# Grouped attention on one core: wide transposes of query and key with a permuted row order, and V loaded dense and spread by GpSimd

## The chip, the cores and the metric

The kernel runs on one core of one Trainium2 chip. The core has five engines that run side by side and meet only at semaphores: TensorE (PE; its weight loads are listed apart as PEld), VectorE (DVE), ScalarE (ACT), GpSimd (POOL) and SyncE (SP), which here only issues DMAs. The metric is the device time of one execution in microseconds (us), as the median of several executions. Two versions of the kernel are told apart by the ratio of their medians.

## The reference

```python
B, Hq, Hkv, Sq, Sk, D = 16, 32, 8, 288, 512, 128      # bf16
def reference(q, k, v):
    k = jnp.repeat(k, Hq // Hkv, axis=1)
    v = jnp.repeat(v, Hq // Hkv, axis=1)
    scores = jnp.einsum("bhqd,bhkd->bhqk", q, k) * D ** -0.5
    p = softmax(scores, axis=-1)
    return jnp.einsum("bhqk,bhkd->bhqd", p, v)
```

Four query heads share one key/value head. So there are 16 x 8 = 128 independent groups, each with 4 x 288 = 1152 query rows against 512 keys of 128 numbers. The softmax is taken without subtracting a maximum; a flag at the end says whether the sums stayed in range, and a slow general path would run if they had not.

## The kernel before

The program goes through the 128 groups one after the other. Two sizes name everything: `NT = 9` is the number of 128-row tiles of the 1152 queries of a group, `NJ = 4` the number of 128-key tiles of its 512 keys.

**Loads.** Four groups make a unit (`UG = 4`, so 32 units), and three units fit in SBUF (`NSLOT = 3`). `op_load` (lines 377 to 399) issues three DMAs for a unit on the queue of SyncE: a transposing DMA for the keys (line 388), one for the queries (line 391), and a plain one for V (line 398). The transposes read rows of 128 numbers that lie one behind the other in HBM and leave, on 128 partitions (the 128 numbers of a row), the columns in the order of the rows: `qt_sb[:, slot, group, 0:1152]` and `kt_sb[:, slot, group, 0:512]`. The plain load writes V in pieces of 128 numbers (256 bytes) into rows of 160 (`VP = 160`), of which column 128 holds a one. From the fourth unit on, `op_load` first waits until the S products and the PV products of the unit that had the slot are done. The first unit is loaded in two parts, its first group by itself, so that work can begin early; its V comes behind the second part.

**S products.** The scores are made transposed: keys on partitions, queries along the free axis. For each group, 4 key tiles x 1152 queries make 4608 columns, cut into three steps of 1536 columns. `op_s` (line 429) does one step, by four matmuls of up to 512 columns whose weights are a 128x128 tile of `kt_sb` and whose moving operand is a stretch of `qt_sb`. The step's result fills one of two PSUM buffers `ps_s`.

**Exponentials.** `op_exp` (line 460) reads the 1536 columns of one step from `ps_s` and writes them, as bf16, to `pt_sb`, which holds three groups. There are 384 of these steps, all on ScalarE.

**PV products.** `op_pv` (line 447) does one third of a group: three query tiles, each the sum of four matmuls over the key tiles. Here the exponentials are the weights (128 keys x 128 queries), and V with its column of ones is the moving operand, 129 columns; column 129 of the result is the softmax's denominator. Because the output rows are stored as `(p t)`, so that each partition writes nine neighbouring rows, tile `t` takes the queries t, t+9, t+18, ... of the group, and the 128 weights of a row are read from `pt_sb` with a step of nine elements (line 446).

**Division and stores.** VectorE takes the reciprocals of the three denominators (line 468) and multiplies (line 480) into `o_sb`, which holds six groups. `op_store` (line 405) sends a finished group to HBM, on SyncE's queue again.

**Order.** TensorE's order is written out by hand: for each step n it does the S product of step n and then the PV product of step n - 4 (`LAG = NC + 1 = 4`). The S product of step n waits for the exponential of step n - 2 (its PSUM buffer), the PV product for its group's exponentials and for VectorE's emptying of its PSUM buffer. SyncE's order is a list sorted by keys, in which the loads of a unit come right after the PV products that free its slot and the stores between them. GpSimd has no work in this path.

Of the kernel before, what the change touches and what calls it, by code (L numbers as in the profile page):

```python
# [8 lines left out]
BF16 = mybir.dt.bfloat16  # L9
# [276 lines left out]
def bass_standalone__gqa_softmax__near_ridge_kernel(  # L286
# [5 lines left out]
):  # L292
    B, Hq, Sq, D = q.shape
    _, Hkv, Sk, _ = k.shape
    P = 128
    R = (Hq // Hkv) * Sq
    NJ = Sk // P
    NT = R // P
# [7 lines left out]
    NC = COLS // CH  # L306
    assert COLS % CH == 0 and NT % 3 == 0 and NC == NT // 3
    scale = float(D) ** -0.5
    DV = D + 1
    VP = 160  # L310
    LAG = NC + 1
    UG = 4
    NU = NG // UG
    NSLOT = 3
    NPT = 3
    NO = 6

    q_v = q.rearrange("b h s d -> (b h s) d")
    k_v = k.rearrange("b g s d -> (b g s) d")
    v_v = v.rearrange("b g (j p) d -> p (b g j) d", p=P)  # L320
    o_v = out.rearrange("b h s d -> (b h s) d").rearrange("(g p t) d -> g p (t d)", p=P, t=NT)

    with ExitStack() as es:
        sem = {}

        def S(name):
            if name not in sem:
                sem[name] = es.enter_context(nc.semaphore(name))
            return sem[name]

        flag_i = es.enter_context(nc.sbuf_tensor("flag_i", [1, 1], I32))
        block = es.enter_context(nc.Block())
        main = ExitStack()
        v_sb = main.enter_context(nc.sbuf_tensor("v_sb", [P, NSLOT, UG * NJ, VP], BF16))
        qt_sb = main.enter_context(nc.sbuf_tensor("qt_sb", [P, NSLOT, UG, R], BF16))
        kt_sb = main.enter_context(nc.sbuf_tensor("kt_sb", [P, NSLOT, UG, Sk], BF16))
        pt_sb = main.enter_context(nc.sbuf_tensor("pt_sb", [P, NPT, COLS], BF16))
        o_sb = main.enter_context(nc.sbuf_tensor("o_sb", [P, NO, NT, D], BF16))
        rl_sb = main.enter_context(nc.sbuf_tensor("rl_sb", [P, NG * NT], FP32))
# [3 lines left out]
        dum = main.enter_context(nc.sbuf_tensor("dum", [P, 2], FP32))  # L343
# [5 lines left out]
        def need(eng, waits):  # L349

            left = []
            for (s, n) in waits:
                key = (id(eng), s)
                if seen.get(key, 0) < n:
                    seen[key] = n
                    left.append((sem[s], n))
            return left

        def emit(eng, waits, fn):
            waits = need(eng, waits)  # L360
            for (s, n) in waits[:-1]:
                eng.wait_ge(s, n)
            ins = fn()
            if waits:
                ins.wait_op(waits[-1][0], waits[-1][1], "sem-ge")
            return ins

        for name in ["s_one", "s_s", "s_e", "s_pv", "s_rc", "s_ev", "s_stat", "s_bad", "s_flag", "s_go", "s_q0", "s_k0"]:
            S(name)
        for i in range(NSLOT):  # L370
            for name in ["s_q%d", "s_k%d", "s_v%d"]:
# [5 lines left out]
        def op_load(u, part=None):  # L377
            eng = nc.sync
            sl = u % NSLOT
            if u >= NSLOT:  # L380
                last = (u - NSLOT + 1) * UG - 1
                for (s, n) in need(eng, [("s_s", NC * (last + 1)), ("s_pv", NC * (last + 1))]):
                    eng.wait_ge(s, n)
            g0, g1 = {None: (0, UG), 0: (0, 1), 1: (1, UG)}[part]
            sq = sem["s_q0"] if part == 0 else sem["us_q%d" % sl]
            sk = sem["s_k0"] if part == 0 else sem["us_k%d" % sl]
            gg = u * UG
            eng.dma_start_transpose(  # L388
                kt_sb[:, sl, g0:g1].rearrange("d g c -> d (g c)"),
                k_v[(gg + g0) * Sk:(gg + g1) * Sk]).then_inc(sk, 16)  # L390
            eng.dma_start_transpose(  # L391
                qt_sb[:, sl, g0:g1].rearrange("d g c -> d (g c)"),
                q_v[(gg + g0) * R:(gg + g1) * R]).then_inc(sq, 16)
            if part != 0:
                if u == 0:
                    for (s, n) in need(eng, [("s_one", 1)]):
                        eng.wait_ge(s, n)
                eng.dma_start(
                    v_sb[:, sl, :, 0:D], v_v[:, gg * NJ:(gg + UG) * NJ]).then_inc(sem["us_v%d" % sl], 16)

        def op_store(g):
            eng = nc.sync
# [5 lines left out]
        def pieces(i):  # L408
            cuts = sorted({i * CH, (i + 1) * CH}
                          | {x for x in range(0, COLS, BANK) if i * CH < x < (i + 1) * CH}  # L410
                          | {x for x in range(0, COLS, R) if i * CH < x < (i + 1) * CH})
            return list(zip(cuts[:-1], cuts[1:]))

        def op_s(n):
            eng = nc.tensor
            g, i = n // NC, n % NC
            u, gi = g // UG, g % UG
            sl = u % NSLOT
            waits = []
            if g == 0:  # L420
                waits += [("s_k0", 16), ("s_q0", 16)]
            else:
                waits += [("us_k%d" % sl, 16 * (u // NSLOT + 1)), ("us_q%d" % sl, 16 * (u // NSLOT + 1))]
            if n >= 2:
                waits.append(("s_e", n - 1))
            ps = pieces(i)
            for x, (a, b) in enumerate(ps):
                j, r0 = a // R, a % R
                ins = emit(eng, waits if x == 0 else [], lambda: eng.matmul(  # L429
                    ps_s[:, n % 2, a - i * CH:b - i * CH],  # L430
                    kt_sb[:, sl, gi, j * P:(j + 1) * P],
                    qt_sb[:, sl, gi, r0:r0 + b - a], start=True, stop=True))
            ins.then_inc(sem["s_s"], 1)

        def op_pv(r):
            eng = nc.tensor
            g = r // NC
            u, gi = g // UG, g % UG
            sl = u % NSLOT
            waits = [("us_v%d" % sl, 16 * (u // NSLOT + 1)), ("s_e", NC * (g + 1))]  # L440
            if r >= 2:
                waits.append(("s_ev", r - 1))
            for a in range(3):
                t = 3 * (r % NC) + a
                for j in range(NJ):
                    w = pt_sb[:, g % NPT, j * R:(j + 1) * R].rearrange("k (p t) -> k t p", t=NT)[:, t]
                    ins = emit(eng, waits if a == 0 and j == 0 else [], lambda: eng.matmul(  # L447
                        ps_o[:, r % 2, a * DV:(a + 1) * DV], w,
                        v_sb[:, sl, gi * NJ + j, 0:DV],
                        start=(j == 0), stop=(j == NJ - 1)))  # L450
            ins.then_inc(sem["s_pv"], 1)


        def op_exp(n):
            eng = nc.scalar
            g, i = n // NC, n % NC
            waits = [("s_s", n + 1)]
            if g >= NPT:
                waits.insert(0, ("s_pv", NC * (g - NPT + 1)))
            emit(eng, waits, lambda: eng.activation(  # L460
                pt_sb[:, g % NPT, i * CH:(i + 1) * CH], ps_s[:, n % 2], ACTF.Exp, scale=scale)
            ).then_inc(sem["s_e"], 1)


        def op_rc(r):
# [40 lines left out]
        @block.sync  # L506
        def _(eng):
            for (_, fn) in sp:
                fn()
            for g in range(max(0, NG - NO), NG):  # L510
                for (s, n) in need(eng, [("s_o%d" % (g % NO), 16 * (g // NO + 1))]):
                    eng.wait_ge(s, n)
# [13 lines left out]
        def _(eng):  # L526
            emit(eng, [("s_one", 1)], lambda: eng.activation(dum[:, 1:2], dum[:, 0:1], ACTF.Exp))  # L527
            for n in range(NS):
                op_exp(n)

        @block.vector
        def _(eng):
            eng.memset(dum[:], 0.0)  # L533
            eng.memset(one_f[:], 1.0)
            eng.memset(v_sb[:, :, :, D:VP], 1.0).then_inc(sem["s_one"], 1)  # L535
            per_b = G * NC
            for r in range(NS):
                op_rc(r)
                op_ev(r)
                if r % per_b == per_b - 1:  # L540
                    op_stat(r // per_b)
            emit(eng, [("s_stat", B)], lambda: eng.tensor_reduce(  # L542
                ck_sb[:, 0:1], st_sb[:, 0, :], AX.X, ALU.max))
            eng.tensor_reduce(ck_sb[:, 1:2], st_sb[:, 1, :], AX.X, ALU.min).then_inc(sem["s_stat"], 1)  # L544
            emit(eng, [("s_stat", B + 1)], lambda: eng.tensor_scalar(  # L545
                out=ck_sb[:, 2:3], in0=ck_sb[:, 0:1], scalar1=SUM_MAX, scalar2=None, op0=ALU.is_gt)
            ).then_inc(sem["s_stat"], 1)
            emit(eng, [("s_stat", B + 2)], lambda: eng.scalar_tensor_tensor(  # L548
                out=ck_sb[:, 3:4], in0=ck_sb[:, 1:2], scalar=1.0 / SUM_MAX, in1=ck_sb[:, 2:3],
                op0=ALU.is_lt, op1=ALU.add)).then_inc(sem["s_bad"], 1)  # L550
            emit(eng, [("s_bad", 2)], lambda: eng.tensor_copy(flag_i[:], ps_s[0:1, 0, 0:1])  # L551
                 ).then_inc(sem["s_flag"], 1)
# [52 lines left out]
```

## Time and profile before

| what | us |
|---|---|
| median of 6 runs | 542.43 (542.10 to 543.21) |
| the profiled execution, its own time | 542.57 |
| its span, first to last instruction | 540.8 |
| ScalarE busy | 523.2 (97%) |
| TensorE busy (matmuls) | 520.6 (96%) |
| TensorE weight loads | 427.5 (79%) |
| VectorE busy | 290.2 (54%) |
| GpSimd busy | 0.2 (0%) |
| chain that ended last: share of PE lines 447 and 429 | 51% and 44% |

The granted TensorE clock was 0.996 over the span. A busy share is no proof of a bound: matmuls are pipelined, and an activation's recorded time overlaps the next one's, so that one engine can stand at 97% while it waits a little before every step. What bounds a step is read from the starts of the steps, which the timeline gives. Two rows of the transfers are worth having at hand too: the DMA queue of SyncE's transfers was busy for 88.2% of 16 engines' span, and 283200 of the 299650 packets had under 512 bytes.

### The profile page before, as it was taken

The numbers are of one execution on the slowest core, as the hardware profiler recorded it, in microseconds if no ns is written. First come the engines' busy times: TensorE is split into PE (matmuls) and PEld (weight loads), VectorE is DVE, ScalarE is ACT, GpSimd is POOL, SyncE is SP. The second block draws the span as 40 slices with busy tenths as digits, with TensorE's granted clock in tenths as the row PEclk, the third lists the DMA queues.
The fourth block names the chain that finished last, engine by engine and source line by source line (L and its number), as shares of the span: only waits on it lengthen the run. The fifth ranks groups of instructions, "written<-read, shape, count | busy, mean of one in ns | idle before, by whom it ended". The sixth has DMA issues, their size and how long they took to land.

```text
span 540.8 us, 13994 instructions
## 1 busy us (share of the span) xinstructions
PE 520.6 (96%) x6045; PEld 427.5 (79%) x6146; DVE 290.2 (54%) x808; ACT 523.2 (97%) x386; POOL 0.2 (0%) x4
## 2 busy tenths in 40 slices
PE   4999999999999999999999999999999999999994
PEld 1788888888888888888888888888888888888884
DVE  1455555555555555555555555555555555555554
ACT  4999999999999999999999999999999999999992
POOL 0000000000000000000000000000000000000000
PEclk9999999999999999999999999999999999999998
DMA  8999989988879997999989889998999889799211
GB/s 165 213 245 261 229 217 248 191 216 199 204 208 249 172 223 196 212 218 245 210 177 199 226 213 239 167 224 207 206 228 226 190 197 220 209 230 220 100 67 70
DMA packets 299650, 110.01 MB, mean 203 GB/s; under 512 B 283200, under 2 KB 283200, under 8 KB 299584
## 3 DMA queue, kind: packets, MB, share of 16 engines
q1 hardware_dynamic: 299584, 109.07, 88.2%
q8 instruction: 49, 0.80, 0.7%
q14 instruction: 17, 0.14, 0.1%
HBM read 16.78 MB, written 37.75 MB: 101 GB/s over the span
## 4 chain that ended last, share of the span: by engine, by line
PE 95%; DMA 1%; issue 1%; SPq 1%; DVE 1%
PE ps_o L447 51%; PE ps_s L429 44%; DMA qt_sb<-in_q_dram 1%; SPq L388 1%; DVE o_sb L480 0%; SPq L391 0%; DVE rl_sb L468 0%; PE ps_s L521 0%; DVE ck_sb L548 0%; DVE ck_sb L542 0%; DVE ck_sb L545 0%; DVE flag_i L551 0%; DVE st_sb L492 0%; DVE st_sb L490 0%; DVE ck_sb L544 0%
## 5 line engine op out<-in xcount | busy, mean ns | idle before, releaser
L460 ACT ACTIVATE pt_sb<-ps_s 128x1536 bf16<-128x1536 f32 x384 | 521.7, 1450 | 6.4 <-PE ps_s L429 6.4
L447 PEld LDWEIGHTS ps_o<-v_sb,pt_sb 128*128 128x128 bf16 x4608 | 333.0, 140 | 40.4 <-DMA v_sb<-in_v_dram 0.6
L447 PE MATMUL ps_o<-v_sb,pt_sb 128*128 128x129 bf16 x4608 | 334.5, 222 | 1.6 <-DVE o_sb L480 0.2
L429 PE MATMUL ps_s<-qt_sb,kt_sb 128*128 128x512 bf16 (+3 forms) x1435 | 297.6, 325 | 11.8 <-DMA qt_sb<-in_q_dram 7.6
L480 DVE TENSOR_TENSOR o_sb<-ps_o,rl_sb 128x384 bf16<-128x384 f32 x384 | 214.3, 558 | 13.5 <-DVE rl_sb L468 0.3
L468 DVE RECIPROCAL rl_sb<-ps_o 128x3 f32<-128x3 f32 x384 | 69.6, 181 | 230.8 <-PE ps_o L447 230.8
L429 PEld LDWEIGHTS ps_s<-qt_sb,kt_sb 128*128 128x128 bf16 x1536 | 131.6, 99 | 65.9 <-DMA qt_sb<-in_q_dram 6.1
L492 DVE TENSOR_REDUCE st_sb<-rl_sb 128x1 f32<-128x72 f32 x16 | 3.5, 218 | 0.0
L490 DVE TENSOR_REDUCE st_sb<-rl_sb 128x1 f32<-128x72 f32 x16 | 3.5, 218 | 0.0
L527 ACT ACT_TABLE_LOAD x1 | 1.3, 1283 | 0.8 <-PEq L590 0.8
L521 PE MATMUL ps_s<-ck_sb,one_f 128*1 128x1 f32 x2 | 0.2, 164 | 1.8 <-DVE ck_sb L548 1.8
L521 PEld LDWEIGHTS ps_s<-ck_sb,one_f 128*1 128x1 f32 x2 | 0.1, 80 | 1.9 <-DVE ck_sb L548 1.9
L535 DVE MEMSET v_sb<- 128x1536 bf16 x1 | 1.3, 1338 | 0.3 <-issue 0.3
L527 ACT ACTIVATE dum<-dum 128x1 f32<-128x1 f32 x1 | 0.2, 202 | 0.5 <-DVE v_sb L535 0.5
L533 DVE MEMSET dum<- 128x2 f32 x1 | 0.1, 60 | 0.9 <-PEq L590 0.9
L551 DVE CAST flag_i<-ps_s 1x1 int32<-1x1 f32 x1 | 0.1, 146 | 0.3 <-PE ps_s L521 0.3
L542 DVE TENSOR_REDUCE ck_sb<-st_sb 128x1 f32<-128x16 f32 x1 | 0.2, 170 | 0.0
L548 DVE SCALAR_TENSOR_TENSOR ck_sb<-ck_sb 128x1 f32<-128x1 f32 x1 | 0.2, 159 | 0.0
L545 DVE TENSOR_SCALAR ck_sb<-ck_sb 128x1 f32<-128x1 f32 x1 | 0.2, 153 | 0.0
L544 DVE TENSOR_REDUCE ck_sb<-st_sb 128x1 f32<-128x16 f32 x1 | 0.2, 158 | 0.0
L590 POOL MEMSET const-bfloat16-1.0<- 128x1 bf16 x1 | 0.1, 102 | 0.0
L590 POOL MEMSET const-uint8-127<- 128x1 uint8 x1 | 0.1, 101 | 0.0
(3 smaller groups left out, 0.3 us busy)
## 6 DMA issues: line engine op xcount, KB each, us to landing
out_dram<-o_sb SPq DMA_DIRECT2D x128, 288.0 KB, 4.4
v_sb<-in_v_dram SPq DMA_DIRECT2D x32, 512.0 KB, 5.2
kt_sb<-in_k_dram SPq DMA_TRANSPOSE x33, 4.8
qt_sb<-in_q_dram SPq DMA_TRANSPOSE x33, 8.1
```

Of the source, the lines that this page charges most:

```text
L388: eng.dma_start_transpose(kt_sb[:, sl, g0:g1].rearrange("d g c -> d (g c)"), k_v[(gg + g0) * Sk:(gg + g1) * Sk]).then_inc(sk, 16)
L429: ins = emit(eng, waits if x == 0 else [], lambda: eng.matmul(ps_s[:, n % 2, a - i * CH:b - i * CH], kt_sb[:, sl, gi, j * P:(j + 1) * P], ...
L447: ins = emit(eng, waits if a == 0 and j == 0 else [], lambda: eng.matmul(ps_o[:, r % 2, a * DV:(a + 1) * DV], w, v_sb[:, sl, gi * NJ + j, ...
L460: emit(eng, waits, lambda: eng.activation(pt_sb[:, g % NPT, i * CH:(i + 1) * CH], ps_s[:, n % 2], ACTF.Exp, scale=scale)).then_inc(sem["s_ ...
L468: emit(eng, [("s_pv", r + 1)], lambda: eng.reciprocal(rl_sb[:, 3 * r:3 * r + 3], src.rearrange("p a e -> p (a e)"))).then_inc(sem["s_rc"], 1)
L480: emit(eng, waits, lambda: eng.tensor_tensor(out=o_sb[:, g % NO, t0:t0 + 3, :], in0=src, in1=rl_sb[:, 3 * r:3 * r + 3].unsqueeze(2).broadc ...
L490: emit(eng, [("s_rc", (b + 1) * w // 3)], lambda: eng.tensor_reduce(st_sb[:, 0, b:b + 1], rl_sb[:, b * w:(b + 1) * w], AX.X, ALU.max))
L492: eng.tensor_reduce(st_sb[:, 1, b:b + 1], rl_sb[:, b * w:(b + 1) * w], AX.X, ALU.min).then_inc(sem["s_stat"], 1)
L521: emit(eng, [("s_bad", 1)], lambda: eng.matmul(ps_s[0:1, 0, 0:1], one_f[:], ck_sb[:, 3:4], start=True, stop=True)).then_inc(sem["s_bad"], 1)
L527: emit(eng, [("s_one", 1)], lambda: eng.activation(dum[:, 1:2], dum[:, 0:1], ACTF.Exp))
L535: eng.memset(v_sb[:, :, :, D:VP], 1.0).then_inc(sem["s_one"], 1)
L542: emit(eng, [("s_stat", B)], lambda: eng.tensor_reduce(ck_sb[:, 0:1], st_sb[:, 0, :], AX.X, ALU.max))
```

## The change

The rows of queries and keys are taken in another order, so that what the PV products read as weights lies together.

* The query rows of a group are numbered `x * 9 + t`. The source of the transposing DMA is now read as 128 rows for each group with 9 x 128 = 1152 numbers each, and the result is `qt_sb[:, slot, t, group, 0:128]`. For the keys it is 128 rows of 4 x 128 = 512 numbers, giving `kt_sb[:, slot, j, group, 0:128]`. The number of DMAs and their bytes stay.
* The S products read the moving operand as up to four stretches of 128 elements, one for each tile t.
* The PV weights are `pt_sb[:, ..., j * 1152 + t * 128 : ... + 128]`, 128 neighbouring elements.
* V is loaded into a new tile `vd_sb`, four neighbouring rows (1024 bytes) on each partition and group, and GpSimd copies it (`op_vc`, one copy for each unit, 32 in all) into `v_sb`, whose rows are now 129 wide. The PV products of a unit wait for this copy in place of the DMA.
* The loads of queries and keys of a unit no longer wait for the PV products of the unit that had the slot, only for its S products; the V load waits for the copy that empties `vd_sb`; the copy waits for the PV products that free `v_sb`.
* The column of ones is set by GpSimd, not by VectorE.

```diff
-    VP = 160
+    VP = DV
...
-    q_v = q.rearrange("b h s d -> (b h s) d")
-    k_v = k.rearrange("b g s d -> (b g s) d")
-    v_v = v.rearrange("b g (j p) d -> p (b g j) d", p=P)
+    q_v = q.rearrange("b h s d -> (b h s) d").rearrange("(x t) d -> x (t d)", t=NT)
+    k_v = k.rearrange("b g (p j) d -> (b g p) (j d)", j=NJ)
+    v_v = v.rearrange("b g (p j) d -> p (b g) (j d)", j=NJ)
...
+        vd_sb = main.enter_context(nc.sbuf_tensor("vd_sb", [P, NSLOT, UG, NJ * D], BF16))
         v_sb = main.enter_context(nc.sbuf_tensor("v_sb", [P, NSLOT, UG * NJ, VP], BF16))
-        qt_sb = main.enter_context(nc.sbuf_tensor("qt_sb", [P, NSLOT, UG, R], BF16))
-        kt_sb = main.enter_context(nc.sbuf_tensor("kt_sb", [P, NSLOT, UG, Sk], BF16))
+        qt_sb = main.enter_context(nc.sbuf_tensor("qt_sb", [P, NSLOT, NT, UG, P], BF16))
+        kt_sb = main.enter_context(nc.sbuf_tensor("kt_sb", [P, NSLOT, NJ, UG, P], BF16))
...
-                for (s, n) in need(eng, [("s_s", NC * (last + 1)), ("s_pv", NC * (last + 1))]):
+                for (s, n) in need(eng, [("s_s", NC * (last + 1))]):
...
             eng.dma_start_transpose(
-                kt_sb[:, sl, g0:g1].rearrange("d g c -> d (g c)"),
-                k_v[(gg + g0) * Sk:(gg + g1) * Sk]).then_inc(sk, 16)
+                kt_sb[:, sl, :, g0:g1].rearrange("d j g p -> d j (g p)"),
+                k_v[(gg + g0) * P:(gg + g1) * P]).then_inc(sk, 16)
             eng.dma_start_transpose(
-                qt_sb[:, sl, g0:g1].rearrange("d g c -> d (g c)"),
-                q_v[(gg + g0) * R:(gg + g1) * R]).then_inc(sq, 16)
+                qt_sb[:, sl, :, g0:g1].rearrange("d t g p -> d t (g p)"),
+                q_v[(gg + g0) * P:(gg + g1) * P]).then_inc(sq, 16)
             if part != 0:
-                if u == 0:
-                    for (s, n) in need(eng, [("s_one", 1)]):
+                if u >= NSLOT:
+                    for (s, n) in need(eng, [("s_vc", u - NSLOT + 1)]):
                         eng.wait_ge(s, n)
                 eng.dma_start(
-                    v_sb[:, sl, :, 0:D], v_v[:, gg * NJ:(gg + UG) * NJ]).then_inc(sem["us_v%d" % sl], 16)
+                    vd_sb[:, sl], v_v[:, gg:gg + UG]).then_inc(sem["us_v%d" % sl], 16)
...
-                    kt_sb[:, sl, gi, j * P:(j + 1) * P],
-                    qt_sb[:, sl, gi, r0:r0 + b - a], start=True, stop=True))
+                    kt_sb[:, sl, j, gi, :],
+                    qt_sb[:, sl, r0 // P:(r0 + b - a) // P, gi, :], start=True, stop=True))
...
-            waits = [("us_v%d" % sl, 16 * (u // NSLOT + 1)), ("s_e", NC * (g + 1))]
+            waits = [("s_vc", u + 1), ("s_e", NC * (g + 1))]
...
-                    w = pt_sb[:, g % NPT, j * R:(j + 1) * R].rearrange("k (p t) -> k t p", t=NT)[:, t]
+                    w = pt_sb[:, g % NPT, j * R + t * P:j * R + (t + 1) * P]
...
+        def op_vc(u):
+            eng = nc.gpsimd
+            sl = u % NSLOT
+            waits = [("us_v%d" % sl, 16 * (u // NSLOT + 1))]
+            if u >= NSLOT:
+                waits.append(("s_pv", NC * UG * (u - NSLOT + 1)))
+            emit(eng, waits, lambda: eng.tensor_copy(
+                v_sb[:, sl, :, 0:D], vd_sb[:, sl].rearrange("p g (j d) -> p (g j) d", d=D))
+            ).then_inc(sem["s_vc"], 1)
...
+        @block.gpsimd
+        def _(eng):
+            eng.memset(v_sb[:, :, :, D:DV], 1.0)
+            for u in range(NU):
+                op_vc(u)
+
         @block.vector
         def _(eng):
-            eng.memset(dum[:], 0.0)
+            eng.memset(dum[:], 0.0).then_inc(sem["s_one"], 1)
             eng.memset(one_f[:], 1.0)
-            eng.memset(v_sb[:, :, :, D:VP], 1.0).then_inc(sem["s_one"], 1)
```

## The prediction

> **What bounds the kernel now.** First the page: two engines stand at 96 and 97%, so the shares decide nothing. Its costliest groups give the durations.
>
> ```profile
> L460 ACT ACTIVATE pt_sb<-ps_s 128x1536 bf16<-128x1536 f32 x384 | 521.7, 1450 | 6.4 <-PE ps_s L429 6.4
> L447 PEld LDWEIGHTS ps_o<-v_sb,pt_sb 128*128 128x128 bf16 x4608 | 333.0, 140 | 40.4 <-DMA v_sb<-in_v_dram 0.6
> ...
> L429 PEld LDWEIGHTS ps_s<-qt_sb,kt_sb 128*128 128x128 bf16 x1536 | 131.6, 99 | 65.9 <-DMA qt_sb<-in_q_dram 6.1
> ```
>
> Weight loads with a step of nine elements (L447) take 140 ns, contiguous ones (L429) 99 ns. 384 exponentials at 1450 ns would be 557 us, more than the span of 540.8, so they overlap and their starts must be read. Second, the timeline of TensorE in mid-run (start, length):
>
> ```profile
> 250.97 0.89 PE L447 MATMUL ps_o<-v_sb,pt_sb 128*128 128x129 bf16 x12
> 251.70 0.81 PE L429 MATMUL ps_s<-qt_sb,kt_sb 128*128 128x384 bf16 x4
> 252.35 0.86 PE L447 MATMUL ps_o<-v_sb,pt_sb 128*128 128x129 bf16 x12
> 253.05 0.81 PE L429 MATMUL ps_s<-qt_sb,kt_sb 128*128 128x512 bf16 x4
> 253.70 0.86 PE L447 MATMUL ps_o<-v_sb,pt_sb 128*128 128x129 bf16 x12
> 254.39 0.81 PE L429 MATMUL ps_s<-qt_sb,kt_sb 128*128 128x512 bf16 x4
> ```
>
> From start to start, an S product holds TensorE for 0.65 us (251.70 to 252.35), the three PV products of a group for 0.73, 0.70 and 0.69 us. Steps are thus 1.38, 1.35 and 1.34 us, with no row of waiting between. Third, ScalarE at the same time, two neighbouring exponentials to a row; length less 1.45 is the distance of their starts.
>
> ```profile
> 251.17 2.83 ACT L460 ACTIVATE pt_sb<-ps_s 128x1536 bf16<-128x1536 f32 x2
> ...
> 252.55 2.80 ACT L460 ACTIVATE pt_sb<-ps_s 128x1536 bf16<-128x1536 f32 x2
> ```
>
> 1.38 and 1.35. The exponential at 252.55 starts 0.04 us after its S product ends (251.70 + 0.81 = 252.51): ScalarE waits for TensorE. In the long 1.38 step that wait is real. Fourth, the start of the run, where ScalarE once is not waiting:
>
> ```profile
> 6.14 2.74 PE L429 MATMUL ps_s<-qt_sb,kt_sb 128*128 128x512 bf16 x8 [6.14 <-DMA qt_sb<-in_q_dram]
> 7.63 2.79 ACT L460 ACTIVATE pt_sb<-ps_s 128x1536 bf16<-128x1536 f32 x2 [4.82 <-PE ps_s L429]
> ...
> 12.02 2.72 PE L429 MATMUL ps_s<-qt_sb,kt_sb 128*128 128x512 bf16 x8 [1.41 <-DMA qt_sb<-in_q_dram]
> 14.66 0.81 PEld L447 LDWEIGHTS ps_o<-v_sb,pt_sb 128*128 128x128 bf16 x12 [0.62 <-DMA v_sb<-in_v_dram]
> ```
>
> Both S products are done at 6.14 + 2.74 = 8.88, yet the second exponential starts at 7.63 + 2.79 - 1.45 = 8.97, 0.09 later instead of 0.04. So 1.34 (1.347 in the trace's nanoseconds) is ScalarE's own pace. The kernel stands on two bounds: one step in three is TensorE's (1.38), the other two are equal on both engines. The same rows show that the first PV product waits for V until 14.66.
>
> **What the change removes.** With contiguous weights, TensorE's step is 0.65 plus twelve matmuls of 129 columns. The S rows stream 1536 columns in 0.65 us, 0.423 ns a column, so twelve take 0.66 us if streaming alone counts: a step of 1.31. If the 99 ns load only brings the slow PV product down to the other two, it is 1.35. Either way ScalarE's 1.347 takes over as the bound. The timeline has 381 exponentials in one row of 517.49 us, (517.49 - 1.45) / 380 = 1.358 a step. The gain is 380 x (1.358 - 1.347) = 4.2 us; less 0.1 for a start-up step of 1.456 that the average holds and in which the first PV product made ScalarE wait (it returns below), 4.1. With TensorE's slower bound (1.35 throughout) it is about 3.0. I take 3.9, nearer ScalarE's pace, because the S rows' loads of 99 ns hide behind a matmul of only 128 columns there. The last four PV products come after the last exponentials; at 0.03 to 0.07 us each that is 0.1 more. Sum: -4.0.
>
> The page ScalarE: Activation LUTs of the Trainium skill (section What ACT_TABLE_LOAD costs) speaks against this: 186 ns + 0.833 ns an element, less 93 of overlap, would be 1372 ns a step, ScalarE alone would be slower than the present 1.358, and the sum would hold no gain at all. The recorded 1.347 decides.
>
> **What it adds.** GpSimd's copy of V, 128 x 2048 elements, is between the V load and the PV products, 32 times. For all but the first unit it is hidden: its unit is needed two units (2 x 16.3 us) after the load is issued, and the load lands in 5.2 us (median). Were that cover gone, each copy would cost its whole length. The first copy has no cover. Before, V was in at 14.62, that is 2.65 us after the queries of the first unit's second part (12.0). V's packets grow from 256 to 1024 bytes. The bounds are the 2.65 us of now, and the store rows: stores of 288 KB with 2304-byte packets, issued one behind the other, land 0.7 us apart (48.26, 48.96, 49.65), so 512 KB in 1.25, with the 0.4 us that V now lands after its last packets. I take 1.9 (landed at 13.9), between them and nearer the stores, whose rows are also long runs. The copy itself has no row on GpSimd. Nearest rows: VectorE's memset of 1536 bf16 elements in 1338 ns (0.87 ns each, so 1.8 us) and its multiply of 384 in 558 ns (1.45 ns, so 3.0 us). I take 2.4, the middle, since a copy reads like the one and writes like the other. V is ready at 16.3, 1.7 us later than 14.62. TensorE is in order: behind the waiting PV product stand S step 5 and with it exponential 5, which started at 16.30, or 1.63 after that PV product. It moves by 1.7, and since ScalarE is then the bound, nothing makes it up. Bounds: 13.65 + 1.8 gives +0.8; 14.62 + 3.0 gives +3.0.
>
> The page GPSIMD Engine Reference (section 3.1) has about 1.03 cycles an element at 1.2 GHz for such bodies, an estimate of 1.8 us for the copy and of +1.1 in place of +1.7.
>
> **What it moves.** Bytes and number of the transposes stay, but a 256-byte piece is now read every 2304 (queries) or 1024 bytes (keys). The transfers' rows:
>
> ```profile
> SPq L405 <- DVE o_sb L480: 129.6, 83, 3.7
> SPq L383 <- PE ps_o L447: 78.7, 27, 2.9
> SPq L388 <- PE ps_s L429: 35.1, 29, 2.8
> ...
> v_sb<-in_v_dram SPq DMA_DIRECT2D x32, 512.0 KB, 5.2
> qt_sb<-in_q_dram SPq DMA_TRANSPOSE x33, 8.1
> ```
>
> SyncE's queue waits 243 us for compute, 7.6 a unit, so transfers have room in mid-run. At the start they have none: S step 3 waits until 12.02 for queries issued at 5.00. Lower bound: the same packets at the same pace, 0 (a gain, at most the 1.41 us of that wait, is not excluded by any row). Upper: V's present load reads 256-byte pieces apart and took 2.33 us for 2048 packets, against 14.3 ns for 16 packets in a transpose (18.2 against 14.3, 1.27 times): 7.0 x 0.27 = +1.9 us. I take 0, since the transposes' own row is the nearest.
>
> The page DMA: Bandwidth & Descriptors (section Latency and other measured facts) speaks against it: 261 GB/s with a non-contiguous middle dimension, some 30% under 350 to 400 for a contiguous one. Here the contiguous one already moves 1.18 MB in an issue of 4.63 us, 255 GB/s; a further 30% would put 3.0 us on the start and the sum at 543.3.
>
> Costed at nothing: the loads' dropped wait for PV (they start four steps, 5.4 us, earlier in a queue that waits anyway; the stores behind them have six `o_sb` buffers); V's new wait for a copy two units old; the column of ones moved to GpSimd, 0.1 us beside the first loads; S reading stretches of 128 elements at the same column count. VectorE has 1.35 - 0.74 = 0.6 us of slack a step, should GpSimd's copies touch it.
>
> Sum against the profiled execution: 542.57 - 4.0 + 1.7 = 540.3. The median is 0.14 lower: 540.2.
>
> **Rivals.** (1) The transfers become the bound: slower. For: 88.2% of the DMA engines' time is taken, and 9 of those 14.4 us a unit are transposes (6656 packets x 21.4 ns / 16). Against: the 7.6 us of waiting. It decides between 1.9 and 7.6 us more a unit; at twice the transposes' issue time of 6.7 us, with 0.9 back from V and a room of 4.5, it adds 1.3 x 29 units: 578. Chance 0.09. (2) The first unit's short transposes suffer: 128 and 384 wide rows spread worse over 16 DMA engines than 1152 and 3456 narrow ones. Twice 7.0 us for the second part is +5 to +7, so 545 to 547; against it, bytes are the same. 0.10. (3) ScalarE or TensorE does not gain: V's rows are now 258 bytes apart, which no row shows as a moving operand, and ScalarE's 1.347 is seen free of waiting only at the start. Then only the 1.7 is left: 544. Two of three steps at 1.35 speak for it, the 99 ns against. 0.13. (4) GpSimd's copies stop VectorE's emptying of PSUM: 32 x (2.4 - 0.6) = +58, so 598; against, VectorE reads but one small operand from SBUF. 0.04. (5) The change doesn't do what it says, contiguous weights loading no faster: that is rival 3's number.
>
> **Numbers.** The forecast has 0.64: its own range is 538.2 (V at +0.8 in place of +1.7, and 1.1 of the 1.41 us given back by the transposes) to 543.4 (V at +3.0, transposes at +1.9). Within 0.2% (1.1 us, what a measurement tells from no change) lie 541.3 to 543.5. Of the 0.64, 0.50 is faster, 0.10 the same, 0.04 slower; rival 3 gives 0.01, 0.05 and 0.07, rival 2 0.01, 0.01 and 0.08, the others are slower. So 0.52, 0.16 and 0.32. The range reaches to rivals 2 and 3: 538.2 to 546.5.
>
> **What would show it.** Right: L447 weight loads near 99 ns, exponentials 1.347 apart in all steps, PE rows with a wait for ACT before S, the first PV product near 16.4 behind the copy. Wrong: queue waits gone from SPq, S waiting for queries beyond 12.0, or a PV product still over 0.69.

## The result, and the profile after

The change made the kernel slightly slower: 544.63 us (median of 20 runs, 542.50 to 545.57) against 542.57 (41 runs of the kernel before, beside them), a ratio of 1.0029 with a 95% interval of 1.0021 to 1.0038, that is, by 2.1 us. 540.2 was predicted.

First the changed kernel's page: its span, rows of the costliest groups (busy us, mean ns of one, idle time before them), and two of the DMA issues (the last number is the median us to landing).

```profile
span 543.2 us, 14127 instructions
...
L462 ACT ACTIVATE pt_sb<-ps_s 128x1536 bf16<-128x1536 f32 x384 | 520.4, 1451 | 10.6 <-PE ps_s L431 10.6
L449 PEld LDWEIGHTS ps_o<-v_sb,pt_sb 128*128 128x128 bf16 x4608 | 301.1, 98 | 58.7 <-POOL v_sb L473 3.3
...
L473 POOL COPY v_sb<-vd_sb 128x2048 bf16<-128x2048 bf16 x32 | 60.7, 1896 | 440.7 <-DMA vd_sb<-in_v_dram 326.7
...
vd_sb<-in_v_dram SPq DMA_DIRECT2D x32, 512.0 KB, 4.9
...
qt_sb<-in_q_dram SPq DMA_TRANSPOSE x33, 8.5
```

The PV weights (L449) now load in 98 ns, where they took 140. The copy takes 1.90 us. The transposes land in 8.5 us (8.1 before). What the faster weight loads should have bought is read from TensorE's timeline in mid-run (start, length):

```profile
251.29 0.87 PE L449 MATMUL ps_o<-v_sb,pt_sb 128*128 128x129 bf16 x12
251.99 0.81 PE L431 MATMUL ps_s<-qt_sb,kt_sb 128*128 128x512 bf16 x4
252.64 0.87 PE L449 MATMUL ps_o<-v_sb,pt_sb 128*128 128x129 bf16 x12
253.35 0.81 PE L431 MATMUL ps_s<-qt_sb,kt_sb 128*128 128x512 bf16 x4
253.99 0.87 PE L449 MATMUL ps_o<-v_sb,pt_sb 128*128 128x129 bf16 x12
254.70 0.60 PE L431 MATMUL ps_s<-qt_sb,kt_sb 128*128 128x384 bf16 x3
```

A PV product holds TensorE for 0.70 to 0.71 us, all three alike. The slow one (0.73) is gone, but the two others got no faster, they rather lost 0.01. There is no wait for ACT in these rows: TensorE is the bound of every step now. The long row of exponentials gives the step:

```profile
99.81 430.75 ACT L462 ACTIVATE pt_sb<-ps_s 128x1536 bf16<-128x1536 f32 x318
```

(430.75 - 1.45) / 317 = 1.354 us a step. Before it was (517.49 - 1.45) / 380 = 1.358, from this row of the kernel before:

```profile
13.49 517.49 ACT L460 ACTIVATE pt_sb<-ps_s 128x1536 bf16<-128x1536 f32 x381 [1.40 <-PE ps_s L429]
```

In the trace's nanoseconds 3.5 ns are gained, which is 1.3 us over 380 steps. The loss lies at the start, in the timeline of the first units (changed kernel):

```profile
12.38 1.46 PE L431 MATMUL ps_s<-qt_sb,kt_sb 128*128 128x512 bf16 x8 [1.79 <-DMA qt_sb<-in_q_dram]
...
14.79 1.89 POOL L473 COPY v_sb<-vd_sb 128x2048 bf16<-128x2048 bf16 x1 [13.68 <-DMA vd_sb<-in_v_dram]
...
16.74 1.31 PE L449 MATMUL ps_o<-v_sb,pt_sb 128*128 128x129 bf16 x12 [2.90 <-POOL v_sb L473]
...
17.84 1.49 PE L431 MATMUL ps_s<-qt_sb,kt_sb 128*128 128x384 bf16 x4
...
19.36 1.45 ACT L462 ACTIVATE pt_sb<-ps_s 128x1536 bf16<-128x1536 f32 x1 [3.35 <-PE ps_s L431]
...
21.26 4.16 ACT L462 ACTIVATE pt_sb<-ps_s 128x1536 bf16<-128x1536 f32 x3 [0.45 <-PE ps_s L431]
```

The same places in the kernel before, where exponential 6 is the second of the last row and starts at 16.30 + 2.80 - 1.45:

```profile
14.67 0.94 PE L447 MATMUL ps_o<-v_sb,pt_sb 128*128 128x129 bf16 x12
...
16.30 2.80 ACT L460 ACTIVATE pt_sb<-ps_s 128x1536 bf16<-128x1536 f32 x2
```

The first PV product starts at 16.74 instead of 14.67, behind the copy. Then its matmuls, and those of the next S product (1.49 us where 0.81 is usual), run slowly: two windows of the stretch show it (us from:to, length, busy time and instructions of PE, PEld, DVE, ACT and POOL, granted clock, DMA share, GB/s).

```profile
16.70:19.00 2.30, 2.26 (x16) 1.67 (x17) 0.74 (x2) 0.00 (x0) 0.00 (x0) 0.56 1.13 223
19.00:21.00 2.00, 2.00 (x17) 1.64 (x16) 0.35 (x2) 1.45 (x1) 0.00 (x0) 0.65 1.28 290
```

The granted clock is 0.56 and 0.65 there (in the clock records of the trace, 0.50 from 16.99 to 20.40 and 1.00 on both sides). Exponential 6, counted from 0, starts at 21.26, against 17.64 before: 3.6 us are lost, 2.07 waiting for V and some 1.5 in the low clock. So the profile's sum is +3.6 - 1.3 = +2.3, and the spans say 543.2 - 540.8 = +2.4.

### The profile page after: what moved, and what is told of

Same layout as the page of the kernel before. It is cut to its first block, busy times and chain, and to the rows that moved or that the text cites. A ratio compares the mean times of both kernels' runs of the same rounds, so it can differ in the third digit from the quotient of the medians.

```text
span 543.2 us, 14127 instructions
## 1 busy us (share of the span) xinstructions
PE 524.5 (97%) x6146; PEld 411.2 (76%) x6146; DVE 288.7 (53%) x807; ACT 521.9 (96%) x386; POOL 61.2 (11%) x37
## 4 chain that ended last, share of the span: by engine, by line
PE 95%; SPq 2%; DMA 1%; DVE 1%; POOL 0%; issue 0%
PE ps_o L449 50%; PE ps_s L431 45%; SPq L393 1%; DMA vd_sb<-in_v_dram 1%; SPq L390 1%; POOL v_sb L473 0%; DVE o_sb L493 0%; DVE rl_sb L481 0%; PE ps_s L534 0%; DVE ck_sb L560 0%; DVE ck_sb L566 0%; DVE ck_sb L563 0%; DVE flag_i L569 0%; DVE st_sb L505 0%; DVE st_sb L503 0%
## 5 line engine op out<-in xcount | busy, mean ns | idle before, releaser
L449 PEld LDWEIGHTS ps_o<-v_sb,pt_sb 128*128 128x128 bf16 x4608 | 301.1, 98 | 58.7 <-POOL v_sb L473 3.3
L449 PE MATMUL ps_o<-v_sb,pt_sb 128*128 128x129 bf16 x4608 | 333.9, 221 | 3.3 <-POOL v_sb L473 2.9
L431 PE MATMUL ps_s<-qt_sb,kt_sb 128*128 128x512 bf16 (+3 forms) x1536 | 313.8, 327 | 8.5 <-DMA qt_sb<-in_q_dram 8.2
L431 PEld LDWEIGHTS ps_s<-qt_sb,kt_sb 128*128 128x128 bf16 x1536 | 130.0, 98 | 66.0 <-DMA qt_sb<-in_q_dram 6.4
L473 POOL COPY v_sb<-vd_sb 128x2048 bf16<-128x2048 bf16 x32 | 60.7, 1896 | 440.7 <-DMA vd_sb<-in_v_dram 326.7
```

What stands on the lines that cost most here:

```text
L473: emit(eng, waits, lambda: eng.tensor_copy(v_sb[:, sl, :, 0:D], vd_sb[:, sl].rearrange("p g (j d) -> p (g j) d", d=D))).then_inc(sem["s_vc ...
```

## The experiments

Two things are to be explained: why contiguous weights, loading 42 ns faster, bought only 1.3 us, and why the start lost 3.6. For the first the theory was V's new row length, 258 bytes in place of 320 (rival: GpSimd's copies or the new S operand slow the matmuls); for the second the copy alone (rival: the low clock after TensorE's idling, which work in the gap would prevent). Each run's ratio is to the kernel before, run beside it.

**V's rows 320 bytes apart again, all else as changed.**

```diff
-    VP = DV
+    VP = 160
```

> The changed kernel with V's rows in v_sb 160 elements (320 bytes) apart in place of 129 (258 bytes), nothing else. In the changed kernel the PV matmuls of key tiles 1 to 3 start 59 to 61 ns after one another and those of key tile 0 56 ns; steps are 1.354 us. Theory (row pitch): a moving operand that starts off an 8-byte boundary costs TensorE 3 to 5 ns. Then all twelve start 56 ns apart, PV products take 0.675 us, ScalarE becomes the bound at 1.347 to 1.348 a step and the run is 380 x 0.0065 = 2.5 us shorter than the changed kernel, some 542.0; the start stays as late. Rival (accumulation): key tiles 1 to 3 add to PSUM and are slower for that. Then the distances stay at 59 to 61 and the time at 544.5.

Measured: 540.5 us (6 runs), ratio 0.9947 (0.9926 to 0.9967). The steps, from the row of exponentials:

```profile
98.41 431.63 ACT L462 ACTIVATE pt_sb<-ps_s 128x1536 bf16<-128x1536 f32 x321
```

(431.63 - 1.77) / 320 = 1.343 (1.77 is the recorded length of the last one, which grows when ScalarE is the bound; see the end). This one number of the layout takes 4 us off the changed kernel. PV products take 0.683 us, and S products now start 0.055 us after the end of the exponential two steps back (0.41 in the changed kernel): ScalarE is the bound. The start stayed as bad (first PV product at 16.84).

**The query part alone.** Wide query transposes and contiguous PV weights; keys, V and waits as before.

```diff
-    q_v = q.rearrange("b h s d -> (b h s) d")
+    q_v = q.rearrange("b h s d -> (b h s) d").rearrange("(x t) d -> x (t d)", t=NT)
...
-        qt_sb = main.enter_context(nc.sbuf_tensor("qt_sb", [P, NSLOT, UG, R], BF16))
+        qt_sb = main.enter_context(nc.sbuf_tensor("qt_sb", [P, NSLOT, NT, UG, P], BF16))
...
-                    w = pt_sb[:, g % NPT, j * R:(j + 1) * R].rearrange("k (p t) -> k t p", t=NT)[:, t]
+                    w = pt_sb[:, g % NPT, j * R + t * P:j * R + (t + 1) * P]
```

> The kernel before with the query part of the change alone: wide query transposes, contiguous PV weights, S reading four stretches of 128. Keys, V (straight into rows of 160, no copy) and all waits as before. Theory: the change's loss is V's path (copy and pitch), its gain the contiguous weights. Then steps are 1.347 us, the start is 0.3 us later than before at most, and the run takes 542.5 - 4.0 + 0.3 = 538.8. Rival (wide transposes or stretched S reads cost the gain): steps stay at 1.354 or more and the run takes 541 to 543.

Measured: **536.79 us** (4 runs), ratio 0.9883 (0.9862 to 0.9904), the fastest version here; it beats both kernels. TensorE in mid-run:

```profile
251.47 0.84 PE L447 MATMUL ps_o<-v_sb,pt_sb 128*128 128x129 bf16 x12
252.16 0.82 PE L429 MATMUL ps_s<-qt_sb,kt_sb 128*128 128x512 bf16 x4
252.82 0.84 PE L447 MATMUL ps_o<-v_sb,pt_sb 128*128 128x129 bf16 x12
...
98.54 427.60 ACT L460 ACTIVATE pt_sb<-ps_s 128x1536 bf16<-128x1536 f32 x318
```

From start to start a PV product and what TensorE waits behind it take 0.68 to 0.69 us, and the last row gives (427.60 - 1.77) / 317 = 1.343 a step. Contiguous weights, with the wide query transposes that they need here, are worth 5.8 us.

**The copy alone.** V goes through a dense tile and GpSimd, as in the change, with V's order, the transposes and the weights of before.

```diff
...
-                    v_sb[:, sl, :, 0:D], v_v[:, gg * NJ:(gg + UG) * NJ]).then_inc(sem["us_v%d" % sl], 16)
+                    vd_sb[:, sl], v_v[:, gg * NJ:(gg + UG) * NJ]).then_inc(sem["us_v%d" % sl], 16)
...
+            emit(eng, waits, lambda: eng.tensor_copy(
+                v_sb[:, sl, :, 0:D], vd_sb[:, sl])
+            ).then_inc(sem["s_vc"], 1)
...
```

> The kernel before with the copy alone: V is loaded as before but into a dense tile, and GpSimd copies it to the rows of 160; transposes, key and query order and strided weights as before. Theory: the copy costs only at the start: the first PV product waits for V and then 1.9 us of copy, TensorE stands idle 2.5 us or more and its clock is granted at about half for some 3 us after that; 542.5 + 2 to 3.6 = 544.5 to 546, with steps of 1.358 in mid-run. Rival (copies disturb VectorE or TensorE in mid-run): steps longer than 1.358 wherever a copy runs, more than 0.1 us a copy, 546 or more.

Measured: 545.73 us (6 runs), ratio 1.0053 (1.0036 to 1.0070), 3.2 us slower. A row of the start, and the row of exponentials:

```profile
15.98 0.95 PE L448 MATMUL ps_o<-v_sb,pt_sb 128*128 128x129 bf16 x12 [3.02 <-POOL v_sb L472]
...
99.35 431.88 ACT L461 ACTIVATE pt_sb<-ps_s 128x1536 bf16<-128x1536 f32 x318
```

TensorE waits 3.02 us for POOL; the steps are (431.88 - 1.45) / 317 = 1.358, as before. The copies cost at the start only; the 31 later ones slow nothing.

**TensorE kept busy until V is there.** Into the changed kernel, ahead of the first PV product, go 13 matmuls of 512 columns whose result nothing uses.

```diff
+                if n == LAG:
+                    for x in range(13):
+                        eng.matmul(ps_o[:, 1, 0:BANK], kt_sb[:, 0, 0, 0, :],
+                                   kt_sb[:, 0, 0, :, :], start=True, stop=True)
```

> The changed kernel with thirteen matmuls of 512 columns added between S step 4 and the first PV product; their result (in the second ps_o buffer) is never read. They fill 2.8 us of the wait for V's copy. Theory (cold clock): TensorE's idle time there is what lowers its granted clock to 0.56 and 0.65 in the 4 us that follow; with the clock kept up, exponentials 5 and 6 come 1.0 and 1.5 us earlier, and the run is about 1.5 us shorter than the changed kernel, 543.0. Rival: the late start is all waiting for V and the copy, the clock is by chance; no change, or up to 0.3 us more.

Measured: 544.63 us (12 runs), ratio 1.0030 (1.0018 to 1.0041), as the changed kernel. From the timeline:

```profile
14.00 4.49 PE L534 MATMUL ps_o<-kt_sb 128*128 128x512 bf16 x13
...
14.63 1.89 POOL L473 COPY v_sb<-vd_sb 128x2048 bf16<-128x2048 bf16 x1 [13.52 <-DMA vd_sb<-in_v_dram]
...
18.32 0.86 PE L449 MATMUL ps_o<-v_sb,pt_sb 128*128 128x129 bf16 x12
```

And windows of it, with the columns of above:

```profile
10.24:13.65 3.41, 1.41 (x10) 0.70 (x9) 0.00 (x0) 2.02 (x3) 0.00 (x0) 1.00 1.03 248
...
14.00:16.70 2.70, 2.70 (x8) 1.05 (x7) 0.00 (x0) 2.17 (x2) 1.89 (x1) 0.50 0.92 206
...
17.06:20.47 3.41, 3.41 (x36) 2.40 (x35) 0.74 (x2) 0.59 (x1) 0.00 (x0) 1.00 1.23 269
```

Most of the added matmuls ran at a clock of 0.50, with no gap before them, and so the first PV product started 1.8 us after V's copy was done (14.63 + 1.89 = 16.52); it ran at full pace. The slow stretch came all the same, only earlier, and exponential 6 started at 21.23 as without them. So work in this gap gained nothing. But it does not clear TensorE's idling of the low clock: the low stretch (13.65 to 17.06 in the clock records) began while the added matmuls were only starting, and behind 3.41 us in which TensorE, waiting for queries, had worked 1.41. In the changed kernel it begins at 16.99, behind as long a stretch in which TensorE had waited for V:

```profile
13.58:16.99 3.41, 0.51 (x7) 0.26 (x6) 0.00 (x0) 2.44 (x2) 1.89 (x1) 1.00 0.98 203
```

All five traces with a stretch at 0.50 near the start have this order; two of them, the query part alone and its 264-byte rows, have no copy at all. Each stretch is 3.41 us long, or twice that, and before each TensorE had worked 0.51 to 1.43 us of 3.41. Where it had worked 1.46 or more of such a stretch (eight cases at full clock near the start), the clock stayed up. The margin between 1.43 and 1.46 is thin, and no run varied the work by itself, so this is a pattern in the records and not a tested cause.

**The query part with 258-byte rows,** to have the row length without any copy.

```diff
-    VP = 160
+    VP = 129
```

> The kernel with the query part alone (e2: 536.8 us), V's rows 129 elements (258 bytes) apart instead of 160, loaded by DMA straight into them, without any copy. Theory (row pitch alone): PV matmuls of key tiles 1 to 3 again 59 to 61 ns apart, steps 1.354, 380 x 0.011 = 4.1 us more: 540.9. Rival (the pitch only mattered together with GpSimd's writes): distances stay at 56.6 ns and the time at 536.8, unless the DMA's writes are late, which would show as waits for V.

Measured: 541.44 us (11 runs), ratio 0.9979 (0.9969 to 0.9990): of the 5.8 us gained by the query part, 0.8 are left, so the row length alone costs 5.0 here by the medians. Steps are 1.354, as in the changed kernel, which is 11 ns x 380 = 4.2 of it; the rest is within the intervals.

**The first unit's copy in four pieces,** on the changed kernel with 320-byte rows: the first PV product waits for its group's quarter only.

```diff
...
-            waits = [("s_vc", u + 1), ("s_e", NC * (g + 1))]
+            waits = [("s_vc", gi + 1 if u == 0 else u + UG), ("s_e", NC * (g + 1))]
...
+            for (a, b) in ([(i, i + 1) for i in range(UG)] if u == 0 else [(0, UG)]):
...
```

> The changed kernel with pitch 160 (e1: 540.5 us) and the first unit's copy cut in four, one for each group, so that the first PV product waits for 512 elements of copy and not for 2048. Theory (the first copy is the rest of the loss against e2, which is 3.7 us): the first PV product starts 1.4 us earlier, and the run takes 540.5 - 1.4 = 539.1, down to 538 if TensorE's clock also stays up more often. Rival (late V load or the clock alone): no change, 540.5.

Measured: 537.79 us (6 runs), ratio 0.9917 (0.9901 to 0.9932). Its start:

```profile
14.63 2.28 POOL L474 COPY v_sb<-vd_sb 128x512 bf16<-128x512 bf16 x4 [13.52 <-DMA vd_sb<-in_v_dram]
15.29 0.85 PE L449 MATMUL ps_o<-v_sb,pt_sb 128*128 128x129 bf16 x12 [1.20 <-POOL v_sb L474]
```

V is in at the usual time, but the PV product starts 0.66 us after the first piece begins, not 1.94. No slow stretch followed in this profile (exponential 6 at 18.18). Against each one's own baseline it gains 4.5 us, where the same kernel with one copy gained 2.1 and the version without any copy 5.8.

**Contiguous weights with the transposes of before:** the permuted order is taken where the S product reads its moving operand, with a step of nine elements.

```diff
-                    qt_sb[:, sl, gi, r0:r0 + b - a], start=True, stop=True))
+                    qt_sb[:, sl, gi].rearrange("d (x t) -> d t x", t=NT)[:, r0 // P:(r0 + b - a) // P], start=True, stop=True))
...
```

> The kernel before with its transposes, keys and V untouched; the permuted order of the queries is made where S reads them, with a step of nine elements in the moving operand, so that the PV weights are contiguous as in the change. Theory (only contiguous PV weights matter for the gain, wide transposes have no part in it): if TensorE streams a moving operand with that step at full pace, steps are 1.343 and the time is 536.5. Rival (a step of nine costs the moving operand as it cost the weights): S products take longer than 0.65 us and the time is over 542.

Measured: 1572.71 us (4 runs), ratio 2.8979 (2.8928 to 2.9031). The timeline shows both sorts of matmul:

```profile
251.38 1.48 PE L447 MATMUL ps_o<-v_sb,pt_sb 128*128 128x129 bf16 x12
252.65 2.97 PE L429 MATMUL ps_s<-qt_sb,kt_sb 128*128 128x384 bf16 x4
255.44 0.83 PE L447 MATMUL ps_o<-v_sb,pt_sb 128*128 128x129 bf16 x6
```

The S product holds TensorE for 255.44 - 252.65 = 2.79 us, 4.3 times 0.65. Not all of this is the step of nine. The PV product in the first row, which has contiguous weights and rows of 320 bytes, also takes 252.65 - 251.38 = 1.27 us, against 0.68 with the query part alone: TensorE went at half its pace here until the clock's first record at 1561.88 us. (Ahead of a trace's first record the views print a clock of 1.00; in every trace here the matmuls before it run at half pace.) At that pace a contiguous matmul of 512 columns takes 427 ns, as at the start of each run; with the step of nine it takes 929, or 2.2 times. Whether the step also brought the half pace on was not tried. Either way contiguous weights cost far more than they gain when they are had this way; of the two ways tried only the wide transposes pay. Having ScalarE write its result in the permuted order was not tried.

**264-byte and 272-byte rows with the query part** (one run each): in 258-byte rows the key tiles of one group differ.

```diff
-    VP = 160
+    VP = 132      # 264 bytes; in the other run 136, 272 bytes
```

> As e5 with rows 132 elements (264 bytes) apart, a multiple of 8 bytes but of no higher power of two. If alignment to 8 bytes is enough, the PV matmuls are 56.6 ns apart as with 160; if 16 or 32 bytes are needed, key tiles 1 to 3 or 1 and 3 are slower, as with 129.

> As e8 with rows 136 elements (272 bytes, 17 x 16) apart. With 264 bytes the key tiles 1 and 3 were slow (59 to 61 ns) and 0 and 2 were not (56 ns); 2 x 264 is a multiple of 16. If a start on a multiple of 16 bytes is what counts, all tiles are at 56.6 ns now, PV takes 0.683 us and TensorE waits for ScalarE as in e2. If 32 or 64 bytes count, key tiles 1 and 3 are slow still.

Measured: 539.52 and 537.35 us. What decides is the distance, in the trace, from the start of a PV matmul to the next start in its product, as a mean over the run for each key tile j, here with the last run's beside it:

```
rows of V              j=0    j=1    j=2    j=3   ns
258 bytes (changed)    56.1   60.4   59.2   59.4
258, query part alone  56.1   60.5   59.2   59.4
264                    56.4   60.0   55.8   59.0
272                    56.7   56.7   56.7   56.7
320                    56.7   56.7   56.7   56.7
264, begun 8 later     56.8   56.1   60.4   55.8
```

Places are counted from the start of V's tile. 272 is 17 x 16 and 320 is 20 x 16: every row begins on a multiple of 16 bytes, and none is slow. With 264, j=1 and j=3 begin 8 bytes off such a multiple and are slow, j=2 (528 = 33 x 16) is not.

**258-byte rows in the kernel before,** strided weights and all.

> The kernel before with V's rows 129 elements apart in place of 160 and nothing else: strided PV weights, V loaded straight into the rows. Theory (each matmul lasts as long as the slower of its weight load's distance and its moving operand): key tiles 1 to 3 go to 59 to 61 ns at least, PV products from 0.73, 0.70 and 0.69 to 0.74, 0.71 and 0.71, steps to 1.367 on average, the time to 542.4 + 380 x 0.009 = 546. Rival (the two add up): 3 ns more on nine matmuls of each product, steps 1.385, the time 552.

Measured: 547.0 us (4 runs), ratio 1.0091 (1.0072 to 1.0111). Its exponentials:

```profile
99.15 431.42 ACT L460 ACTIVATE pt_sb<-ps_s 128x1536 bf16<-128x1536 f32 x315
```

(431.42 - 1.45) / 314 = 1.369 a step, 11 ns over before, 4.2 us in 380 steps. The row length costs about as much with strided weights, so it is no effect of the contiguous ones.

**264-byte rows that begin 8 bytes later,** query part alone (one run).

```diff
-    VP = 160
+    VP = 132
...
-        v_sb = main.enter_context(nc.sbuf_tensor("v_sb", [P, NSLOT, UG * NJ, VP], BF16))
+        v_all = main.enter_context(nc.sbuf_tensor("v_sb", [P, NSLOT, UG * NJ * VP + 8], BF16))
+        v_sb = v_all[:, :, 4:4 + UG * NJ * VP].rearrange("p s (r e) -> p s r e", e=VP)
```

> Wide query transposes alone, V's rows 264 bytes apart as in the run of that pitch, but the whole tile of V begins 8 bytes later, so that key tiles 1 and 3 of a group now begin on a multiple of 16 bytes and key tiles 0 and 2 do not. If the place of a row against 16 bytes sets the pace of a PV matmul: tiles 1 and 3 follow in 56 to 57 ns (they took 60 and 59), tile 2 in 59 to 60 (it took 55.8), and tile 0 in 56 if the overwriting first matmul is exempt, in about 60 if it is not. If instead the number of the key tile in the accumulation or the pitch alone sets it, the four distances stay at 56.4, 60.0, 55.8, 59.0. Time 537.5 to 539.5 in either case; the distances decide.

Measured: 538.28 us, and the last line of the table above. Key tiles 1 and 3, now on a multiple of 16 bytes, are fast, key tile 2, now 8 off, is slow: the slow ones changed places with nothing but the address. Key tile 0 is 8 off and fast. It alone overwrites its PSUM region where the others add to it, and so it seems to be exempt; that this is the reason was not tried by itself.

## Why the prediction was wrong

Against each run's own baseline the parts come to: query part with contiguous weights -5.8, 258-byte rows +5.0 (the same run with and without them), the rest of the change +2.9 (changed kernel, +2.1, against the query part with 258-byte rows, -0.8). The copy measured alone, +3.2, accounts for that rest within its interval.

* **"What the change removes" is the step that failed.** It had TensorE's step fall to 1.31 or 1.35, "Either way ScalarE's 1.347 takes over as the bound", and 4.0 us of gain. It priced the PV matmuls by columns and weight loads alone and took their moving operand to be as before, though the same diff moved V's rows from 320 to 258 bytes. In its place: key tiles 1 to 3 take 59 to 60.5 ns for 56.7, TensorE stays the bound at 1.354, and the gain is 1.3. The prediction's own sign of being wrong, "a PV product still over 0.69", is there: 0.70 to 0.71. Rival 3 named these rows as an operand "which no row shows", at 0.13. That its 544 lies 0.6 from the measured time is partly luck: it had no gain in the steps and 1.7 us of loss at the start, where 1.3 were gained and 3.6 lost.
* **Within that step, a size too.** ScalarE's own pace was read as 1.347 at the start; sustained it is 1.343. And TensorE's step without the bad rows is 0.65 + 12 x 0.0567 = 1.33, between the two values named. So contiguous weights alone were worth 5.8, not 4.0.
* **"What it adds" had the mechanism right and the size wrong.** V landed 2.4 us after the queries (predicted 1.9), the copy took 1.90 us (2.4); with queries 0.36 later this gave +2.07 for the first PV product, near the 1.7 by luck, since the two misses of 0.5 cancel. The low clock after it then took another 1.5. In the kernel before TensorE is slow too, in the S products at 12.02 (2.72 us for 8 matmuls that take 1.46 at 12.38 in the changed kernel): that trace's first clock record, of 1.00, is at 14.66, about when V lands, and so the slow pace costs little. The prediction read that row without seeing that it was slow, and had no term for the clock.
* The estimate of 1.8 us for the copy, worked out from the page GPSIMD Engine Reference of the Trainium skill (section 3.1), was nearer to the measured 1.90 than the 2.4 taken from VectorE's rows.
* **"What it moves": 0 held nearly.** First queries 0.27 us later (6.41 against 6.14), those of the second part 0.36. The 3.0 us estimated from the 30% that the skill's page DMA: Bandwidth & Descriptors (section Latency and other measured facts) gives for a non-contiguous middle dimension are not seen.
* **Costed at nothing, rightly:** the 31 later copies (mid-run steps unchanged with the copy alone, and with that rival 4 fell) and the dropped wait. Rival 1 fell: SyncE's queue still waits 198.7 + 45.9 = 245 us for compute, two rows of the changed kernel's waits (us in total, times, longest):

```profile
SPq L407 <- DVE o_sb L493: 198.7, 87, 3.7
SPq L390 <- PE ps_s L431: 45.9, 29, 4.4
```

* Rival 2 fell with the second part's queries, 0.36 us later and not 5 to 7; rival 5 with the 98 ns.
* The 1372 ns a step worked out from the skill's page ScalarE: Activation LUTs (section What ACT_TABLE_LOAD costs) are contradicted again: 1.343 us is sustained over more than 300 steps.

Still open is the cause of the low-clock stretch near the start. The records only show that it follows 3.41 us in which TensorE had little work, and so its place moved with the waits for queries and V; that more work ahead of the waits would keep it away was not tried.

## What to carry to other kernels

When a diff tightens a padded tile, check what the pad did for its reader: here rows of a moving operand that begin on multiples of 16 bytes are worth 4 to 5 us of 542. Price an operation that the change touches on all of its operands, the unchanged-looking one too, and give a layout that no row of the trace shows a price, not a remark among the rivals. A copy that is hidden 31 times still costs its whole length, and what follows from it, where an in-order engine first waits for it; cutting that first one into the pieces that its readers need gets most of it back (537.79 us here, against 540.5 with one copy). And before a row is taken for an operand's price, see whether TensorE ran at its full pace in it.

## What the runs showed of the hardware

* With contiguous weights and at full clock, a PV matmul of 129 columns that adds to PSUM takes 59 to 60.5 ns from start to start instead of 56 to 57 if its moving row does not begin on a multiple of 16 bytes of V's tile; the overwriting first one does not.
* Strided weights (step of nine) load in 140 ns, contiguous ones in 98; a moving operand with a step of nine takes 2.2 times as long as a contiguous one at the same, halved pace (929 against 427 ns for 512 columns). The page SBUF — State Buffer of the Trainium skill (section Door 1: The DMA port swizzle) agrees in kind: it gives lines of 16 bytes, full bandwidth with two reads to a line, and a step of up to 8 bf16 elements free; nine elements are 18 bytes, a new line for each. It gives no price, and its rule does not yield the first point: 129 elements touch 17 such lines whether they begin on a line or 8 bytes off it.
* An exponential's recorded time is no measure of ScalarE's pace: where ScalarE is the bound, the rows grow from 1450 to 1767 ns while one ends every 1343. In this row of the query part alone one exponential stands by itself:

```profile
251.68 1.77 ACT L460 ACTIVATE pt_sb<-ps_s 128x1536 bf16<-128x1536 f32 x1
```

* In every trace here matmuls take about twice their time until the trace's first clock record (427 ns for 512 columns against 216 after it). That record lies at 9 to 22 us (14.66 in the kernel before, 10.16 in the changed one), and at 1561.88 with the strided queries. The views print 1.00 ahead of it, so a granted clock of 1.00 there does not show full pace. The later slow stretches, of 3.41 us or twice that, are recorded as 0.50.
